# A feed-forward pair on one Trainium2 core: the second product in seven block products, its operand through DRAM

## The chip, the cores and the metric

The kernel runs on one core of a Trainium2 chip. The metric is the device time of one execution in microseconds (us). The engines are named as in the profile: PE is TensorE's matmul, PEld its weight load, DVE is VectorE, ACT ScalarE, POOL GpSimd, SP SyncE, which here issues all DMAs.

## What is computed

Three layers, one after the other, over 4 batches of 576 tokens and 512 channels: block-causal attention, a token and channel mixing layer with sines, and a low-rank layer with a feed-forward pair. The last layer is the one that the change touches:

```python
def _moe2_ref(x, U, V, w_ch1, w_ch2):
    xt = x.transpose(0, 2, 1)
    h = xt @ U @ V
    u = x + h.transpose(0, 2, 1)
    ch = np.maximum(u @ w_ch1, 0.0) @ w_ch2     # 512 -> 2048 -> 512
    return (u + ch).astype(np.float32)
```

`u` has 2304 tokens in all, `w_ch1` is 512 x 2048 and `w_ch2` 2048 x 512. The weights come as 64-bit floats, and each is decoded on the chip from its two 32-bit words.

## The kernel before

**Precision.** A factor of a matmul is held as two parts, a rounded high part and the rest (both fp32r, four bytes). A product of two factors is three matmuls: high by high, high by low, low by high. So the feed-forward pair costs, for every 128 x 128 block of a weight, three matmuls over the tokens.

**Stages.** For batch after batch the kernel runs attention (tiles `s`, `P`, `t`, `oA`, `oB`), then `theta` (`th`), `product` (`xp`), `mix` (`y`), `chan` (`c`), `lowrank` (`xq`, `G`) and `expand` (`h`). `expand` writes the finished `u`, transposed, to DRAM (`u3d`). The stages of one batch are woven into the attention of the next. The feed-forward pair comes last, and its first part fills the stages of the last batch, where no attention is left to weave in.

**The feed-forward pair.** Tokens are cut into five chunks of 512, 256, 512, 512, 512 (`CHUNKS`), hidden units into 16 tiles of 128 (`NF`). `ff1(n, f)` makes the hidden tile `m` of chunk n: 4 channel blocks by 3 matmuls, 12 in all, into one PSUM bank; ACT writes its rectified, rounded value and DVE the rest (`hh`). `ff2(n, f)` takes `hh` at once: 4 output blocks by 3 matmuls into four banks `acc`, which gather over all 16 f. So `m` and `acc` alternate, 12 matmuls each, and the hidden layer never leaves the chip. That makes 960 matmuls for each of the two products: 768 over 512 tokens and 192 over 256. At the end of a chunk POOL rebuilds u (`o`), DVE adds `acc`, and SP sends it out.

**Weights.** `load_f` brings a tile of either weight (`raw_w`, 512 KB), decodes it with two ACT and two DVE instructions of 512 columns (`d_w`), and splits it in two (`w`). All 32 tiles are on the chip before chunk 1 begins, in memory that attention, theta and mix have left.

**What sets the order.** The order is not written by hand. Every step gets a due time (`at_time`, with the table `CFG`), and a list scheduler (`Line.run`, with a price for each instruction in `Line.price`) simulates the engines, gives out buffers (`Line.home`, `fits`) and picks on each engine the ready step that is due first. `plan` repeats this with new priorities and keeps the best end. Some steps may go to one of several engines (`either`), and the scheduler picks one. `keep_warm` then puts dummy transposes (`t<-ident`, without a `P`) where the scheduled PE would idle in the first 140 us. The program on the chip follows the five resulting lists, each engine in its own order, so every recorded instruction bears the line of the recorder, L1195.

## Time and profile before

| | before |
|---|---|
| timed runs, median of 3 (lowest, highest) | 860.24 us (858.26, 861.49) |
| profiled execution, first to last instruction | 857.3 us |
| PE busy | 837.4 us, 98% of the span |
| DVE / ACT / POOL busy | 421.6 / 369.9 / 250.7 us |
| moved by DMA | 57.18 MB, 67 GB/s over the span |

The profile gives no time of the profiled execution besides its span. A share of busy time is a mean over the stages; the slices and windows below show it stage by stage. A PE matmul's duration in a group is the time from its start to its modelled end, and neighbours overlap, so the rate of PE is read from the chain of waits, where a piece such as "x12" spans from its first matmul's start to the next piece's start.

### The profile page before, as it was taken

Reading aid. Unit: us, or ns where it says so; the run is one execution under the profiler, and the core shown is the slowest. Engines: PE = TensorE matmul, PEld = TensorE weight load, DVE = VectorE, ACT = ScalarE, POOL = GpSimd, SP = SyncE. Lnnn points to the kernel's source line nnn. Section 1 sums busy time; section 2 is a strip of 40 time slices with the busy share of each in tenths; the row PEclk is TensorE's granted clock in tenths of the full one; section 3 lists DMA queues with packets and bytes.
Section 4 is the critical chain, followed back from the end, with each engine's and each line's share of the span. In section 5 each row is a group of like instructions: output and inputs, shape, how many; then the busy total and the mean of one; then the engine's idle time right before and its main releaser. Section 6 shows DMA issues by size and latency. Waiting matters only on the chain.

```text
span 857.3 us, 12606 instructions
## 1 busy us (share of the span) xinstructions
PE 837.4 (98%) x4882; PEld 687.3 (80%) x4882; DVE 421.6 (49%) x813; ACT 369.9 (43%) x856; POOL 250.7 (29%) x272
## 2 busy tenths in 40 slices
PE   8989899999999999999999999999999999999998
...
GB/s 216 189 171 114 107 58 59 45 45 30 101 31 31 45 16 57 107 134 83 160 84 105 196 99 0 154 2 75 1 0 1 50 1 0 1 50 0 1 1 49
DMA packets 41595, 57.18 MB, mean 67 GB/s; under 512 B 4672, under 2 KB 25664, under 8 KB 41536
## 3 DMA queue, kind: packets, MB, share of 16 engines
...
## 4 chain that ended last, share of the span: by engine, by line
PE 86%; DVE 6%; ACT 4%; DMA 1%; issue 1%; POOL 1%; SPq 0%; DVEq 0%; POOLq 0%; ACTq 0%
PE acc L1195 23%; PE m L1195 23%; PE y L1195 13%; PE c L1195 6%; PE th L1195 6%; PE t L1195 4%; PE s L1195 4%; PE oB L1195 3%; ACT P L1195 2%; DMA raw_th<-w_theta 1%; PE oA L1195 1%; PE G L1195 1%; DVE nm L1195 1%; PE xp L1195 1%; DVE P L1195 1%
## 5 line engine op out<-in xcount | busy, mean ns | idle before, releaser
L1195 PE MATMUL acc<-hh,w 128*128 128x512 f32 (+1 forms) x900 | 204.2, 373 | 0.5 <-DVE o L1195 0.2
L1195 PE MATMUL m<-us,w 128*128 128x512 f32 (+1 forms) x900 | 202.2, 372 | 0.0
L1195 PEld LDWEIGHTS acc<-hh,w 128*128 128x128 f32 x900 | 156.9, 188 | 32.9 <-DVE o L1195 1.5
L1195 DVE SCALAR_TENSOR_TENSOR hh<-m,hh 128x512 fp32r<-128x512 f32 (+1 forms) x80 | 50.9, 636 | 268.8 <-ACT hh L1195 268.8
L1195 PEld LDWEIGHTS m<-us,w 128*128 128x128 f32 x900 | 156.6, 188 | 30.3
L1195 ACT ACTIVATE hh<-m 128x512 fp32r<-128x512 f32 (+1 forms) x80 | 44.4, 554 | 297.4 <-PE m L1195 292.5
L1195 PE MATMUL y<-wtok,zh 128*128 128x288 f32 x576 | 120.4, 302 | 0.1
L1195 PEld LDWEIGHTS y<-wtok,zh 128*128 128x128 f32 x576 | 92.5, 189 | 4.0 <-issue 1.1
L1195 ACT ACTIVATE P<-s,nm 128x128 f32<-128x128 f32 (+2 forms) x144 | 79.0, 554 | 38.3 <-DVE nm L1195 36.8
L1195 PE MATMUL y<-wtok,zl 128*128 128x288 f32 x288 | 84.7, 297 | 0.0
L1195 PE MATMUL t<-ident,P 128*128 128x128 f32 x400 | 66.0, 284 | 10.1 <-ACT P L1195 3.3
L1195 PEld LDWEIGHTS t<-ident,P 128*128 128x128 f32 x400 | 47.3, 143 | 25.7 <-ACT P L1195 5.7
L1195 DVE TENSOR_REDUCE nm<-s 128x2 f32<-128x256 f32 (+4 forms) x80 | 64.1, 806 | 4.6 <-ACT P L1195 1.8
L1195 PE MATMUL s<-k,q 64*128 64x128 f32 (+4 forms) x320 | 64.9, 451 | 0.2 <-ACT P L1195 0.2
L1195 PE MATMUL c<-u,wch 128*128 128x288 f32 x384 | 59.1, 301 | 0.9 <-DVE xT L1195 0.9
L1195 PEld LDWEIGHTS c<-u,wch 128*128 128x128 f32 x384 | 53.4, 188 | 4.1 <-DVE xT L1195 1.9
L1195 POOL TENSOR_TENSOR o<-us,us 128x512 f32<-128x512 f32 x16 | 20.7, 1320 | 122.4 <-DVE o L1195 84.1
L1195 DVE TENSOR_TENSOR xT<-y,xT 128x288 f32<-128x288 f32 x64 | 29.0, 454 | 51.7 <-PE y L1195 51.4
L1195 PEld LDWEIGHTS y<-wtok,zl 128*128 128x128 f32 x288 | 53.9, 188 | 0.2
L1195 PE MATMUL th<-wth,xh 128*128 128x512 f32 x160 | 50.8, 399 | 0.1
L1195 PEld LDWEIGHTS s<-k,q 64*128 64x128 f32 (+1 forms) x320 | 30.4, 187 | 13.0 <-issue 7.1
L1195 ACT COPY PTB<-t 128x512 f32<-128x512 f32 (+3 forms) x63 | 27.7, 457 | 28.9 <-PE t L1195 28.2
...
## 6 DMA issues: line engine op xcount, KB each, us to landing
...
raw_tok<-wtokT SPq DMA_DIRECT2D x18, 288.0 KB, 3.2
...
k<-kT SPq DMA_DIRECT2D x16, 288.0 KB, 3.4
u3d<-xT SPq DMA_DIRECT2D x16, 288.0 KB, 2.1
outT<-o SPq DMA_DIRECT2D x16, 256.0 KB, 2.0
raw_th<-w_theta SPq DMA_DIRECT2D x8, 256.0 KB, 5.4
```

Source lines behind the costliest of these rows:

```text
L1195: fn(*[place(x) for x in args], **{k: place(x) for k, x in kw.items()})
```

## The change

`ff1` now works on one batch b (576 tokens) and a pair j of hidden tiles (eight pairs). The pair's output is seen as 2 x 2 blocks: two hidden tiles by two halves of 288 tokens. Each block is 12 matmuls over 288 tokens, a plain product. ACT or DVE rectify the blocks; DVE and POOL form the seven sums of blocks that the seven-product scheme (Strassen's, in Winograd's form) wants on the side of h. All seven, as plain fp32, go to DRAM (`hd`, 1.03 MB for each b and j, in four DMAs).

`load_w2` likewise forms the four sums on the side of w2 and splits all seven blocks of a pair of w2's tiles.

`ff2(b, s, j)` reads blocks of `hd` back (`hr`), splits them into two parts on the chip (`hv`) and multiplies: four products for s = 0 and three for s = 1, each 2 x 3 matmuls over 288 tokens. All eight PSUM banks hold the sums of one batch. `leave` combines them with u as each group of products ends. Counts: `ff1` has 4 x 8 x 48 = 1536 matmuls over 288 tokens, `ff2` 4 x 8 x 42 = 1344. The weights w1 are read in the fill as before, w2 only during the later `ff1`. All `ff2` steps come after all `ff1` steps.

```diff
-NA = 11
-CH = 384
-NCH = NT // CH
+NJ = NF // 2
+HW = DM // 2
...
-CFG = dict(L=60., d0=0., d1=0.84, d2=1.0, dec=1.8, T=13.68, P=13.88, R=25.74, I=29.568, X=2.61, m0=4., m1=72.64, w1=1., w2=2., w3=0.2, wx=24., po=0.5)
+CFG = dict(L=60., d0=0., d1=0.84, d2=1.0, dec=1.8, T=13.68, P=13.88, R=25.74, I=29.568, X=2.61, m0=4., m1=80., w1=1., w2=2., w3=0.2, u0=3., f1=150., f2=177., v0=0., v1=140.)
-LOC1 = "BBKKXTTTRRRRRRRB"
-LOC2 = "BBKKXTTTTTTKKKKB"
-CHUNKS = [512, 256, 512, 512, 512]
+NU = 4
+UX = (1,)
+EJ = 5
+NTW = 5
-LOOSE = {"pm": 1, "pa": 1, "hp": 1}
+LOOSE = {"pm": 1, "pa": 1, "F": 3, "G": 6}
-SLOWER = 1000.0
+SLOWER = {"-": 1000.0, "load_w1": 1000.0, "load_w2": 1000.0, "make_u": 300.0, "ff1": 300.0, "ff2": 300.0}
...
+    h3 = [[dram.tile([P, 7 * SH], F32, name=f"hd{b}_{j}") for j in range(NJ)] for b in range(B)]
...
+    for tag, n in {"U": NU, "W": NB, "G": NRX}.items():
+        for i in range(n):
+            line.home("w1p", f"{tag}e{i}", **{tag: ALL})
+    for i in range(4):
+        line.home("ps3", f"F{i}", F=ALL)
+        line.home("pp", f"pm{i}", pm=("s0",), F=("s0", "pm"))
+        line.home("ps", f"pa{i}", pa=(), F=("pa",))
...
     def load_w1(f):
+        t = line.tile([P, 2, DM], F32R, "W", f"w1_{f}")
+        w1t[f] = [t[:, a].rearrange("p (c f) -> p c f", c=NC4) for a in range(2)]
+        d = rawslot(f"d_w1_{f}")[:, :DM]
+        for g in range(2):
+            raw = rawslot(f"raw_w1_{f}_{g}")[:, :DM]
+            nc.sync.dma_start(raw.rearrange("p (c f) -> p c f", c=2), w1src[:, 2 * g:2 * g + 2, 2 * f * P:2 * (f + 1) * P])
+            unpack(raw, d[:, g * HW:(g + 1) * HW])
+        rnd("dh", t[:, 0], f32(d))
+        sub(t[:, 1], f32(d), t[:, 0], "dl")
...
+    def load_w2(j):
+        D = [halves(f"w2v{j}_{k}", U32, w=HW, tag="raw") for k in range(2)]
+        for k in range(2):
+            f = 2 * j + k
+            for v in range(2):
+                raw = rawslot(f"w2raw{j}_{k}{v}")[:, :DM]
+                nc.sync.dma_start(raw, w2[f * P:(f + 1) * P, v * DM:(v + 1) * DM])
+                unpack(raw, D[k][:, v])
+        D = [f32(d) for d in D]
+        sa, sb = [halves(f"w2S{j}_{a}", w=HW, tag="raw") for a in "ab"]
+        tt(sa[:, 0], D[0][:, 1], D[1][:, 1], ALU.add)
+        tt(sa[:, 1], sa[:, 0], D[0][:, 0], ALU.subtract)
+        tt(sb[:, 0], D[0][:, 1], D[0][:, 0], ALU.subtract)
+        tt(sb[:, 1], D[1][:, 0], sa[:, 1], ALU.subtract)
+        dst = wpairs(j)
+        for d, src in zip(dst, (D[0][:, 0:1], D[1], sa, sb)):
+            rnd("wh", d[:, :, 0], src)
+            sub(d[:, :, 1], src, d[:, :, 0])
...
-    def ff1(n, f):
-        u, w = us[n], CHUNKS[n]
-        hp = line.tile([P, 512], F32, "hp", f"m{n}_{f}", PSUM)
-        hp = hp[:, :w]
-        k = 0
-        for c in range(NC4):
-            for g, mv in ((0, 0), (0, 1), (1, 0)):
-                nc.tensor.matmul(hp, w1t[f][g][:, c, :], u[mv][:, c], start=(k == 0), stop=(k == 11))
-                k += 1
-        hh = line.tile([P, 2, max(CHUNKS)], F32R, "hh", f"hh{n}_{f}")[:, :, :w]
-        nc.scalar.activation(out=hh[:, 0], in_=hp, func=AF.Relu)
-        nc.vector.scalar_tensor_tensor(out=hh[:, 1], in0=hp, scalar=0.0, in1=f32(hh[:, 0]),
-                                       op0=ALU.max, op1=ALU.subtract)
-        hs[n, f] = hh
...
-    def ff2(n, f):
-        w = CHUNKS[n]
-        if f == 0:
-            accs[n] = [(abank(f"acc{n}_{d}") if d < PA else line.tile([P, 512], F32, "a3", f"acc{n}_{d}", PSUM))[:, :w]
-                       for d in range(NC4)]
-        hh = hs.pop((n, f))
-        for d in range(NC4):
-            ds_ = slice(d * P, (d + 1) * P)
-            for i, (g, mv) in enumerate(((0, 0), (0, 1), (1, 0))):
-                nc.tensor.matmul(accs[n][d], w2t[f][g][:, ds_], hh[:, mv],
-                                 start=(f == 0 and i == 0), stop=(f == NF - 1 and i == 2))
...
+    FIRST4 = (("A11", "B11", 0), ("S2", "T2", 1), ("S3", "T3", 2), ("S1", "T1", 3))
+    LAST3 = (("A12", "B21", 0), ("A22", "T4", 2), ("S4", "B22", 3))
+
+    def fbank(name):
+        return line.tile([P, 512], F32, "F", name, PSUM)[:, :SH]
+
+    def three(bank_, w, u, start, stop):
+        for i, (g, mv) in enumerate(((0, 0), (0, 1), (1, 0))):
+            nc.tensor.matmul(bank_, w[g], u[mv], start=start and i == 0, stop=stop and i == 2, skip_group_check=True)
+
+    def ff1(b, j):
+        n = f"{b}_{j}"
+        ha, hb, hc, hdd = [halves(f"{x}{n}", tag="G") for x in ("ha", "hb", "hc", "hd")]
+
+        def quarter(k, t):
+            bank_ = fbank(f"m{n}_{k}{t}")
+            w = w1t[2 * j + k]
+            ts_ = slice(t * SH, (t + 1) * SH)
+            for c in range(NC4):
+                three(bank_, [w[g][:, c] for g in range(2)], [uu[b][c][:, g, ts_] for g in range(2)], c == 0, c == NC4 - 1)
+            return bank_
+
+        relu(ha[:, 0], quarter(0, 0))
+        relu(hc[:, 1], quarter(1, 1))
+        m = quarter(0, 1)
+        nc.vector.scalar_tensor_tensor(out=ha[:, 1], in0=m, scalar=0.0, in1=ha[:, 0], op0=ALU.max, op1=ALU.subtract)
+        nc.sync.dma_start(hd[b][j][:, 0:2 * SH].rearrange("p (v c) -> p v c", v=2), ha)
+        nc.vector.scalar_tensor_tensor(out=hb[:, 1], in0=m, scalar=0.0, in1=hc[:, 1], op0=ALU.max, op1=ALU.subtract)
+        tt(hb[:, 0], hc[:, 1], ha[:, 1], ALU.subtract)
+        nc.sync.dma_start(hd[b][j][:, 2 * SH:4 * SH].rearrange("p (v c) -> p v c", v=2), hb)
+        relu(hc[:, 0], quarter(1, 0))
+        nc.sync.dma_start(hd[b][j][:, 4 * SH:6 * SH].rearrange("p (v c) -> p v c", v=2), hc)
+        tt(hdd[:, 0], hc[:, 0], hb[:, 0], ALU.subtract)
+        nc.sync.dma_start(hd[b][j][:, 6 * SH:], hdd[:, 0])
...
+    def ff2(b, s, j):
+        w = wv[j]
+        if s == 0:
+            group, at = FIRST4, ((0, 2, ("B11", "T1")), (2, 4, ("T2", "T3")))
+        else:
+            group, at = LAST3, ((4, 6, ("B21", "B22")), (6, 7, ("T4",)))
+        v = {}
+        for a, c, names in at:
+            k = c - a
+            raw = halves(f"hr{b}_{j}_{a}", n=k, tag="G")
+            nc.sync.dma_start(raw, hd[b][j][:, a * SH:c * SH].rearrange("p (v c) -> p v c", v=k))
+            t = line.tile([P, 2, 2, SH], F32R, "U", f"hv{b}_{j}_{a}")[:, :k]
+            rnd("hh", t[:, :, 0], raw)
+            sub(t[:, :, 1], raw, t[:, :, 0])
+            for i, x in enumerate(names):
+                v[x] = t[:, i]
+        for a, x, k in group:
+            for m in range(2):
+                if s == 0 and j == 0:
+                    accs[b, k, m] = fbank(f"acc{b}_{k}_{m}")
+                three(accs[b, k, m], [w[a][:, g, m * P:(m + 1) * P] for g in range(2)],
+                      [x_ for x_ in (v[x][:, 0], v[x][:, 1])], s == 0 and j == 0, j == NJ - 1)
+            if j == NJ - 1:
+                for m in range(2):
+                    leave(b, s, k, m)
...
+        r, ea, eb = evs[b, m]
+        acc = accs[b, k, m]
+        o11, o12, o21, o22 = [r[h][:, t * SH:(t + 1) * SH] for h in range(2) for t in range(2)]
+        s1, u2, u3, x = ea[:, 0], ea[:, 1], eb[:, 0], eb[:, 1]
+        if s == 0:
+            if k == 0:
+                nc.scalar.copy(s1, acc)
+            elif k == 1:
+                tt(u2, acc, s1, ALU.add)
+                tt(o12, o12, u2, ALU.add)
+                tt(o21, o21, u2, ALU.add)
+            elif k == 2:
+                tt(u3, acc, u2, ALU.add)
+                tt(o22, o22, u3, ALU.add)
+            else:
+                tt(o22, acc, o22, ALU.add)
+        elif k == 0:
+            tt(o11, acc, o11, ALU.add)
+        elif k == 2:
+            tt(o21, acc, o21, ALU.add)
+            nc.sync.dma_start(outT[(2 + m) * P:(3 + m) * P, b * S:(b + 1) * S], r[1])
+        else:
+            tt(o12, acc, o12, ALU.add)
...
+    first = [(b, j) for j in range(EJ) for b in (0, 1)] if MIX else [(b, j) for b in (0, 1) for j in range(EJ)]
+    for i, (b, j) in enumerate(first):
+        when = max(when, t1 + CFG["m1"] * i / len(first), nw[2 * j + 1] + 0.01)
+        feed(b, j, when)
+    t = max(tE, when)
+    late = [(b, j) for b in (0, 1) for j in range(EJ, NJ)] + [(b, j) for j in range(NJ) for b in (2, 3)]
+    for i, (b, j) in enumerate(late):
+        feed(b, j, t + CFG["f1"] * i / len(late))
+    for j in range(NJ):
+        at_time(tE + CFG["v0"] + CFG["v1"] * j / NJ, load_w2, j)
+    t += CFG["f1"]
+    step = CFG["f2"] / B / NJ / 7
+    for b in range(B):
+        for s in range(2):
+            for j in range(NJ):
+                at_time(t, ff2, b, s, j)
+                t += step * (3 if s else 4)
```

The order of the new program at the places that the prediction speaks of:

PE in the fill of the last batch before: `acc` of one hidden tile and `m` of the next alternate, 512 tokens a matmul (`hh` is the split hidden tile, `us` the split u, `w` a weight tile).

```order
L1195 MATMUL acc_0_4659<-hh_8_5599,w_8_5300 128x512 x3
L1195 MATMUL acc_1_4866<-hh_8_5599,w_8_5300 128x512 x3
L1195 MATMUL acc_2_4604<-hh_8_5599,w_8_5300 128x512 x3
L1195 MATMUL acc_3_4639<-hh_8_5599,w_8_5300 128x512 x3
L1195 MATMUL m_10_5675<-us_0_4221,w_10_0_5411 128x512
L1195 MATMUL m_10_5675<-us_1_4251,w_10_0_5411 128x512
L1195 MATMUL m_10_5675<-us_0_4221,w_10_1_5441 128x512
```

Four of the twelve blocks of `m` stand here. Each hidden tile is used as soon as it is split.

PE now, at the one place where `ff1` (`m`, from the split u `uf`) ends and `ff2` (`acc`, from the split blocks `hv` and the blocks of w2 `w2d`, `w2b`, `w2c`) begins.

```order
L1295 MATMUL m_7_10_7987<-uf_0_6836,w_15_5957 128x288 x3
L1295 MATMUL m_7_10_7987<-uf_1_6859,w_15_5957 128x288 x3
L1295 MATMUL m_7_10_7987<-uf_2_6892,w_15_5957 128x288 x3
L1295 MATMUL m_7_10_7987<-uf_3_6909,w_15_5957 128x288 x3
L1295 MATMUL acc_0_0_8013<-hv_0_0_7911,w2d_6001 128x288 x3
L1295 MATMUL acc_0_1_8018<-hv_0_0_7911,w2d_6001 128x288 x3
L1295 MATMUL acc_1_0_8025<-hv_0_2_7919,w2b_6155 128x288 x3
L1295 MATMUL acc_1_1_8030<-hv_0_2_7919,w2b_6155 128x288 x3
L1295 MATMUL acc_2_0_8036<-hv_0_2_7919,w2c_6177 128x288 x3
L1295 MATMUL acc_2_1_8044<-hv_0_2_7919,w2c_6177 128x288 x3
```

What alternated stands apart: 1536 `m` and then, without a break, 1344 `acc`, all of 288 tokens.

PE now, where the four products of the first batch end and the three begin (the last pair j = 7, then j = 0 and one group of j = 1).

```order
L1295 MATMUL acc_2_0_8036<-hv_7_2_8177,w2c_7991 128x288 x3
L1295 MATMUL acc_2_1_8044<-hv_7_2_8177,w2c_7991 128x288 x3
L1295 MATMUL acc_3_0_8051<-hv_7_0_8168,w2b_7857 128x288 x3
L1295 MATMUL acc_3_1_8057<-hv_7_0_8168,w2b_7857 128x288 x3
L1295 MATMUL acc_0_0_8013<-hv_0_4_8202,w2a_6124 128x288 x3
L1295 MATMUL acc_0_1_8018<-hv_0_4_8202,w2a_6124 128x288 x3
L1295 MATMUL acc_2_0_8036<-hv_0_6_8211,w2a_6124 128x288 x3
L1295 MATMUL acc_2_1_8044<-hv_0_6_8211,w2a_6124 128x288 x3
L1295 MATMUL acc_0_0_8013<-hv_1_4_8236,w2x_6591 128x288 x3
L1295 MATMUL acc_0_1_8018<-hv_1_4_8236,w2x_6591 128x288
L1295 MATMUL acc_3_0_8051<-hv_0_4_8202,w2c_6177 128x288 x3
L1295 MATMUL acc_3_1_8057<-hv_0_4_8202,w2c_6177 128x288 x3
```

Between the last matmul that `acc_3` gets from the four products and the next one that writes it stand 16 others: the groups of `acc_0` and `acc_2`, and 4 of the next pair that the scheduler pulled ahead.

DVE now, at the same place: what it does between two runs of splits (`ea`, `eb` hold partial sums, `o` is u on its way to the output).

```order
L1295 TENSOR_TENSOR eb_0_8304<-acc_2_0_8036,ea_0_8284 128x288
L1295 TENSOR_TENSOR eb_1_8309<-acc_2_1_8044,ea_1_8290 128x288
L1295 TENSOR_TENSOR o_1_8082<-o_1_8082,ea_1_8290 128x288
L1295 TENSOR_TENSOR o_3_8089<-o_3_8089,ea_1_8290 128x288
L1295 TENSOR_TENSOR o_2_8073<-o_2_8073,eb_0_8304 128x288
L1295 TENSOR_TENSOR o_3_8089<-o_3_8089,eb_1_8309 128x288
L1295 TENSOR_TENSOR o_2_8073<-acc_3_0_8051,o_2_8073 128x288
L1295 TENSOR_TENSOR o_3_8089<-acc_3_1_8057,o_3_8089 128x288
L1295 TENSOR_TENSOR hv_3_4_8311<-hr_3_4_8184,hv_3_4_8311 128x2x288
L1295 TENSOR_TENSOR hv_4_4_8352<-hr_4_4_8219,hv_4_4_8352 128x2x288
L1295 TENSOR_TENSOR hv_4_6_8372<-hr_4_6_8225,hv_4_6_8372 128x288
L1295 TENSOR_TENSOR hv_5_4_8388<-hr_5_4_8253,hv_5_4_8388 128x2x288
```

The second half of the output work reads `acc_3` behind eight other additions; before the change DVE had four additions at the end of a chunk.

PE before, in the attention of the second batch, after `oB` of its second head pair.

```order
L1195 MATMUL xp_4_1266<-ident,xd_1152 128x128 x4
L1195 MATMUL s_3_2_1277<-k_3_1009,q_3_999 128x384 x2
L1195 MATMUL t_2_0_1_1293<-ident 128x128 x4
L1195 MATMUL t_2_0_0_1298<-ident,P_2_0_1108 128x128
L1195 MATMUL t_2_0_1_1293<-ident 128x128 x2
L1195 MATMUL t_2_0_1_1293<-ident,P_2_0_1108 128x128
L1195 MATMUL t_2_0_0_1298<-ident,P_2_1_1129 128x128 x2
L1195 MATMUL t_2_0_1_1293<-ident,P_2_1_1129 128x128 x2
L1195 MATMUL xp_1_1328<-ident,xT_381 128x128 x4
L1195 MATMUL t_2_2_0_1340<-ident,P_2_2_1167 128x128 x3
```

There are 6 dummy transposes in these rows.

PE now, at the same place.

```order
L1295 MATMUL xp_4_1310<-ident,xd_1194 128x128 x4
L1295 MATMUL s_3_2_1321<-k_3_1048,q_3_1039 128x384 x2
L1295 MATMUL t_2_0_1_1349<-ident 128x128 x21
L1295 MATMUL t_2_0_0_1371<-ident,P_2_0_1161 128x128
L1295 MATMUL t_2_0_1_1349<-ident,P_2_0_1161 128x128
L1295 MATMUL t_2_0_0_1371<-ident,P_2_1_1174 128x128
L1295 MATMUL xp_1_1380<-ident,xT_426 128x128 x4
L1295 MATMUL t_2_0_0_1371<-ident,P_2_1_1174 128x128
L1295 MATMUL t_2_0_1_1349<-ident,P_2_1_1174 128x128 x2
L1295 MATMUL t_2_2_0_1401<-ident,P_2_2_1205 128x128 x3
```

The dummy transposes are now 21 in one piece, and 9 more follow before the first `y`; in the whole program 97 stand where 62 stood. The steps themselves stand in nearly the same order.

## Rows read from the trace of the kernel before

**Rows 1.** The page: busy time of the engines, and 40 slices of the span.

```profile
PE 837.4 (98%) x4882; PEld 687.3 (80%) x4882; DVE 421.6 (49%) x813; ACT 369.9 (43%) x856; POOL 250.7 (29%) x272
PE   8989899999999999999999999999999999999998
GB/s 216 189 171 114 107 58 59 45 45 30 101 31 31 45 16 57 107 134 83 160 84 105 196 99 0 154 2 75 1 0 1 50 1 0 1 50 0 1 1 49
```

**Rows 2.** Busy us by window: start:end, length, engines with (xinstructions), PE clock, DMA share, GB/s.

```profile
480.00:500.00 20.00, 20.00 (x89) 15.49 (x88) 19.31 (x31) 14.90 (x27) 3.07 (x4) 1.00 0.61 193
600.00:650.00 50.00, 50.00 (x216) 40.30 (x215) 6.22 (x9) 5.39 (x9) 0.00 (x0) 1.00 0.00 1
800.00:857.30 57.30, 53.60 (x231) 42.92 (x229) 8.96 (x13) 5.39 (x9) 0.00 (x0) 1.00 0.05 19
```

**Rows 3.** Chain of waits: start us, length us, what; matmuls of 512, 256, 288 columns.

```profile
499.52 2.80 PE m L1195 x12
496.72 2.80 PE acc L1195 x12
...
555.76 1.38 PE acc L1195 x12
557.13 1.42 PE m L1195 x12
...
450.85 6.34 PE c L1195 x48
457.19 6.41 PE y L1195 x48
463.60 3.27 PE c L1195 x24
```

**Rows 4.** Groups by shape, eviction, decode and split: engine, operation, shapes xcount | busy, mean ns | idle.

```profile
L1195 DVE TENSOR_TENSOR xT<-y,xT 128x288 f32<-128x288 f32 x64 | 29.0, 454 | 51.7 <-PE y L1195 51.4
L1195 DVE TENSOR_TENSOR w<-d_w,w 128x512 fp32r<-128x512 f32 x12 | 8.0, 682 | 0.0
L1195 DVE TENSOR_TENSOR us<-u,us 128x512 fp32r<-128x512 f32 x5 | 6.6, 1337 | 2.0 <-PE m L1195 2.0
L1195 DVE TENSOR_TENSOR u<-xT,u 128x288 fp32r<-128x288 f32 x9 | 4.4, 494 | 0.6 <-POOL u L1195 0.6
L1195 DVE SCALAR_TENSOR_TENSOR da_th<-da_th,raw_th 128x256 uint32<-128x256 uint32 x8 | 3.3, 420 | 0.6 <-ACT raw_th L1195 0.6
L1195 DVE TENSOR_TENSOR wtok<-da_tok,wtok 128x576 fp32r<-128x576 f32 x1 | 0.7, 745 | 0.0
L1195 POOL TENSOR_TENSOR w<-d_w,w 128x512 fp32r<-128x512 f32 x18 | 25.6, 1429 | 20.1 <-ACT w L1195 16.9 <-DVE w L1195 3.0
L1195 POOL TENSOR_TENSOR u<-xT,u 128x288 fp32r<-128x288 f32 x23 | 18.9, 824 | 11.5 <-ACT u L1195 5.4 <-DVE u L1195 4.9
L1195 POOL TENSOR_TENSOR o<-us 128x256 f32<-128x256 f32 x4 | 2.9, 738 | 0.0
L1195 ACT ACTIVATE wtok<-da_tok 128x576 fp32r<-128x576 f32 x1 | 0.7, 666 | 0.0
```

**Rows 5.** DMA: two windows as in Rows 2, then issues with KB and us to landing.

```profile
0.00:20.00 20.00, 16.42 (x103) 11.73 (x104) 11.57 (x33) 13.04 (x42) 6.24 (x13) 1.00 0.68 221
548.00:552.00 4.00, 3.92 (x31) 3.50 (x30) 3.76 (x8) 0.77 (x2) 4.00 (x5) 1.00 0.99 350
...
u3d<-xT SPq DMA_DIRECT2D x16, 288.0 KB, 2.1
u<-u3d SPq DMA_DIRECT2D x8, 256.0 KB, 3.3
```

**Rows 6.** The clock's fall: windows as in Rows 2, then PE's row of the timeline.

```profile
100.00:110.00 10.00, 6.70 (x31) 3.75 (x31) 9.67 (x21) 9.07 (x17) 7.37 (x9) 0.69 0.36 118
110.00:120.00 10.00, 9.91 (x65) 9.37 (x63) 8.04 (x16) 8.11 (x23) 6.40 (x7) 0.80 0.08 26
...
104.86 1.39 PE L1195 MATMUL t<-ident,P 128*128 128x128 f32 x4 [2.40 <-DVE P L1195]
```

**Rows 7.** Timeline of the end: start us, length us, engine, what.

```profile
847.89 5.71 PE L1195 MATMUL acc<-hh,w 128*128 128x512 f32 x24
851.64 2.74 DVE L1195 TENSOR_TENSOR o<-acc,o 128x512 f32<-128x512 f32 x4 [2.23 <-PE acc L1195]
852.36 2.38 SPq L1195 DMA_DIRECT2D outT<-o  x4
```

More of the change, by code (lines that the diff above doesn't have):

```diff
@@ L410, in run @@
                     best, f = min((max(t, free[f]) + y.cost, f) for f, y in x.ways.items())
-                    if f != e and best < t + way.cost - SLOWER:
+                    if f != e and best < t + way.cost - x.slow:
                         stash.append(item)
@@ L618, in abank, with wtile @@
         return line.tile([P, 512], F32, "pa", name, PSUM)
-    def wtile(name):
-        return line.tile([P, 2, DM], F32R, "K", name)
+    def wtile(name, tag):
+        return line.tile([P, 2, DM], F32R, tag, name)
     def toktile(name):
@@ L1004, in build @@
         spread(t0, t0 + CFG["X"], [(expand, b, d) for d in range(NC4)])
-    w1src = w1.rearrange("(c p) f -> p c f", p=P)
-    w1t, w2t = [None] * NF, [None] * NF
-    def btile(name, shape, dt):
-        return line.tile(shape, dt, "B", name)
-    def load_f(name, src, oh, ol):
-        raw = btile(f"raw_{name}", [P, 2 * DM], U32)
-        nc.sync.dma_start(raw if len(src.shape) == 2 else raw.rearrange("p (c f) -> p c f", c=NC4), src)
-        ta = rawslot(f"d_{name}", U32)[:, :DM]
-        decode([(raw.rearrange("p (c two) -> p c two", two=2), slice(0, DM))], ta, oh, ol)
@@ L1095, in pre_out @@
[L1095 to L1107 removed]
+    hd = [[line.fixed(h3[b][j], f"hd{b}_{j}") for j in range(NJ)] for b in range(B)]
@@ new lines, in tt, with relu @@
+    def tt(out, a, b, op):
+        if a.space == PSUM:
+            nc.vector.tensor_tensor(out=out, in0=a, in1=b, op=op)
+        else:
+            line.either(lambda: nc.gpsimd.tensor_tensor(out=out, in0=a, in1=b, op=op),
+                        lambda: nc.vector.tensor_tensor(out=out, in0=a, in1=b, op=op))
+    def relu(out, a):
+        line.either(lambda: nc.scalar.activation(out=out, in_=a, func=AF.Relu),
+                    lambda: nc.vector.tensor_scalar(out=out, in0=a, scalar1=0.0, scalar2=0.0, op0=ALU.max, op1=ALU.max))
@@ new lines, in halves, with unpack @@
+    def halves(name, dt=F32, n=2, w=SH, tag="RT"):
+        return line.tile([P, S], dt, tag, name)[:, :n * w].rearrange("p (v c) -> p v c", v=n)
+    w1src = w1.rearrange("(c p) f -> p c f", p=P)
+    w1t = [None] * NF
+    def unpack(raw, ta):
+        r = raw.rearrange("p (c two) -> p c two", two=2)
+        lo, hi = r[:, :, 0], r[:, :, 1]
+        nc.scalar.activation(out=f32(ta), in_=f32(hi), func=AF.Copy, scale=EXPFIX)
+        nc.scalar.activation(out=lo, in_=lo, func=AF.Copy, scale=LOFIX)
+        nc.vector.scalar_tensor_tensor(out=ta, in0=ta, scalar=3, in1=lo,
+                                       op0=ALU.logical_shift_left, op1=ALU.bitwise_or)
+        nc.vector.scalar_tensor_tensor(out=ta, in0=hi, scalar=SIGN, in1=ta,
+                                       op0=ALU.bitwise_and, op1=ALU.bitwise_or)
@@ new lines, in build, with wpairs @@
+    wparts, wv = {}, {}
+    def wpairs(j):
+        q, k = divmod(j, 2)
+        pair = [P, 2, 2, HW]
+        if q in LONE:
+            first = line.tile([P, 1, 2, HW], F32R, "W1", f"w2d{j}")
+        else:
+            if q not in wparts:
+                wparts[q] = line.tile(pair, F32R, "W", f"w2d{q}")
+            first = wparts[q][:, k:k + 1]
+        if j in INX:
+            x = xtile(f"w2x{j}", [P, 2, 2, 2, HW], F32R)
+            mid = [x[:, 0], x[:, 1], line.tile(pair, F32R, "W", f"w2c{j}")]
+        else:
+            mid = [line.tile(pair, F32R, "W", f"w2{a}{j}") for a in "abc"]
+        return first, *mid
@@ L1130, in build @@
[L1130 to L1148 removed]
+    tI = tT + 1.0 + CFG["P"] + CFG["R"]
```

181 lines of the change are left out of this document (72 added, 109 removed).

## The prediction, made before the changed kernel was run

> **What bounds the kernel now.** I read the busy line and the slices first [rows 1]. PE is busy 837.4 us of the span of 857.3, and its slices stand at 9 in all but the first and the last; DVE is busy 421.6 us, ACT 369.9, POOL 250.7. A share over the whole span hides stages, so the windows come next [rows 2]. In 600 to 650 PE is busy 50.00 of 50 us, DVE 6.22, ACT 5.39, POOL 0, and the DMA engines nothing; in 800 to the end it is much the same (53.60 of 57.30 us, with the tail). In 480 to 500, where `mix` and `chan` of the last batch are woven with the first chunk, PE is also full (20.00), and DVE nearly so (19.31). So from about 480 us on the time is the number of PE's matmuls by their rate, and 250 us of three engines lie unused near the end. That is what the change draws on: it pays PE work with DVE, ACT, POOL and DMA work.
>
> **The feed-forward matmuls.** The chain of waits gives the rate at each width [rows 3]. Twelve matmuls of 512 columns take 2.80 us, 233.3 ns each; twelve of 256 take 1.38 or 1.42 us, 115 to 118.8 ns, say 116.7. Before there are 768 `m` and 768 `acc` of 512 columns and 192 and 192 of 256: 1536 x 233.3 + 384 x 116.7 = 403.2 us. After there are 1536 `m` and 1344 `acc`, all of 288 columns. The trace of before has that width in other stages with the same pattern, a new weight load for each matmul: 48 `c` in 6.34 us, 132.1 ns; 48 `y` in 6.41, 133.5; 24 `c` in 3.27, 136.3 [rows 3]. A straight line through the 256 and 512 rows gives 116.7 + 32 x 116.6/256 = 131.2 ns. I take 132.1, the longest full-speed piece: 2880 x 132.1 = 380.4 us, **22.8 less**. The ends are 131.2 ns (377.9, 25.3 less) and 136.3 (392.5, 10.7 less); 133.5 would give 384.5, 18.7 less. Only the second product gets cheaper: an eighth of its half, some 25 us; the narrower matmuls give 2 of that back.
>
> **The new vector work beside `ff1`.** `ff1` and `ff2` now stand apart. The order lets me count what each engine does between the last eviction of `c` and the first `acc`. PE has 1104 `m` there and a few matmuls of `xq`, `G` and `h`, about 152 us. By the groups of before [rows 4], DVE has 63 decodes of 256 words at 420 ns (26.5 us), 52 evictions and rests from PSUM at 454 (23.6), 27 sums of 288 at 494 (13.3), 12 splits at 682 (8.2), and about 20 us in shorter or fewer ones (14 rectifications, 10 more of 420, 8 of 745, 6 from PSUM): 92 us. POOL has 30 at 738, 16 at 824 and 12 at 1429: 52.5 us with two inputs, 7 in others. ACT comes to about 67. None reaches 152, not even DVE and POOL one after the other (144.5). So PE should stay full; for in-order waits within a pair I add **2 us**, between 0 and 8. What hides them is the four `F` banks: PE is a bank or two ahead of the evictions.
>
> **The new vector work beside `ff2`.** PE has 1344 x 0.1321 = 177.5 us. DVE has about 91 splits of 2 x 288 at 745, 48 sums from PSUM at 454, 44 from SBUF at 494: 111 us. ACT has as many roundings at 666 and some copies, about 78 [rows 4]. There are eight `hv` tiles, so the splits run some four pairs ahead. At the join of `ff1` and `ff2` the last `m` and the first `acc` stand back to back; the first `hv` and the last block of w2 are made long before. No term.
>
> **The seams.** Within each of the four batches, at s = 0 to s = 1, the new first write of the bank `acc_3` follows its last one of the four products by 16 matmuls, 16 x 0.1321 = 2.11 us. It is no new start: the three products add onto the same bank only after DVE has taken the old sum away. DVE has by then queued `ea` and `eb` (4 from PSUM at 454), four sums in SBUF at 494, and only then the two that read `acc_3` (454). The last of `acc_2` stands 6 matmuls ahead of the end of `acc_3`, so DVE's four SBUF sums end about 2.2 us after that end, the read of `acc_3_0` about 2.65 after, that of `acc_3_1` about 3.1. PE wants the first at 2.11: a stall of 0.5 to 1 us at each of four seams. **3 us**, between 0 (if the reads go out early) and 6. Behind the reads on DVE stand splits of `hv`, which have four pairs of cover. From batch to batch the next sums take banks that have long been read: 0.
>
> **DMA.** h goes out, 1.03 MB for each of 32 (b, j), 33.0 MB, and comes back, 33.0. In the stretch of `ff1` I count 38.8 MB (h out 23.7, w2 8.4, u 3.5, early reads of h 3.2) in 152 us, 255 GB/s; in `ff2` 39.2 MB (29.8, u again 4.7, output 4.7) in 178 us, 220 GB/s. In the trace of before the queue moved 350 GB/s at a share of 0.99 for 4 us with transfers of the same kind and size, and 221 GB/s at a share of 0.68 for the first 20 us; a 288 KB transfer landed 2.1 us after its issue [rows 5]. By both windows the engines' ceiling is 325 to 350 GB/s, so I take the transfers as hidden, at a share of 0.7 to 0.8. They have no price as long as reads run ahead; the cover is thinner than for any other term.
>
> **The first 400 us.** The steps and their order are the same. The planner fills 97 dummy transposes where it filled 62, 24 of the 35 more at one place, where PE before idled 2.40 us behind DVE's `P` and the clock then stood at 0.69 and 0.80 in two windows of 10 us, which together are some 10 us at the lower level, 1.2 GHz [rows 6]. If the fill keeps PE at 2.4 GHz there, at most 5 us come back; if the dummies are in the way, each for no longer than a matmul of 256 columns [rows 3], 35 x 0.115 = 4 us are lost. I take **1 us less**, between 5 less and 4 more. At the end four evictions and four transfers gave 3.7 us behind the last matmul [rows 7]; now the last are two, of 288 columns, and a transfer of 288 KB: 0.
>
> **Sum.** Against the profiled execution: 857.3 - 22.8 + 2 + 3 - 1 = 838.5. The median of the runs is 2.9 us above that span (860.24 to 857.3), which I carry over: 841.4, **841.5 us**.
>
> **Rivals.**
>
> *DVE becomes the bound of `ff1`.* The split of `us` on DVE beside POOL took 1337 ns, that of `w` of the same size without POOL 682 [rows 4], 1.96 times as long. If that befell every DVE operation with two SBUF inputs there (31.7 us and the decode's 26.5), DVE would have 92 + 56 = 148 us, and with a tenth lost to waits in order 163: some 12 us more than PE's 152, 854. Against it: POOL is busy only 60 of the 152 us, so that the whole factor cannot fall on all. The Trainium skill ("SBUF — State Buffer", section "SBUF: two separate sides") says that a DVE operation with two SBUF inputs and a GpSimd one shut each other out for a whole instruction; by that rule alone the two queues add up to 144.5 us at most and still fit, and the row of 1337 agrees with it.
>
> *The transfers become the bound, slower than before.* If long stretches go no faster than the best slice of before, 216 GB/s [rows 1], `ff1` takes 38.8/0.216 = 179.6 us, 27.6 more, and `ff2` 181.5, 4 more: 873. The point from which it decides is a rate of about 255 GB/s in `ff1`, and it turns slower than before by over 0.5% under some 223 GB/s. For it: SP issues in order, so that a `hd` that waits for DVE holds up reads behind it, and no row shows a rate over 221 for longer than 4 us. Against it: those windows were not short of queue, but of work. The Trainium skill (the same page, section "The DMA setup-cost knee") gives about 2 us for each transfer beside its bytes at 436 GB/s; taken one after another, transfers of 288 KB would run at 110 GB/s by an estimate from that page, and the 78 MB of both stretches would take some 709 us. The window of 350 GB/s contradicts that for several transfers in flight.
>
> *The clock comes back.* The fill works in full and the first part gains 5 us, and the rate is that of the line, 131.2 ns (2.5 us less), with the seams hidden: 841.5 - 4 - 2.5 - 2 = 833.
>
> *The change does not do what it says.* The order settles it: 1536 and 1344 matmuls of 288 columns stand in it.
>
> **How the numbers follow.** The forecast has 0.68, DVE as the bound 0.12, the transfers 0.08, the clock 0.12. Less than 0.5%, 4.3 us, can hardly be told from no change. Faster by more than that (under 855.9) are the forecast, the clock and over half of the DVE case: 0.87. Within 0.5% lies the rest of it: 0.05. Slower (over 864.5) is the transfers' case: 0.08. The range runs from the clock's 833 to 857, which takes in the rate of 136.3 ns (853.5) and the DVE case.
>
> **What would show it.** In the changed profile's chain `m` and `acc` should stand in pieces of x12 with 1.59 us; the first `acc` should begin some 181 us ahead of the end, PE without a gap to its left; ahead of the first new `acc_3` in each batch PE should idle under 1 us behind DVE; the DMA share should be 0.7 to 0.8 in the last 330 us. The forecast is wrong if PE idles in `ff1` behind DVE's or POOL's sums (the first rival), or in either stretch behind `hr` or for a free `ha` to `hd` tile (the second), or if the windows after 100 us show the lower clock at another place than before.

## The result

The changed kernel takes 850.25 us (median of 4 runs, 847.5 to 852.07), the kernel before, in the same comparison, 859.68 (median of 4, 858.26 to 861.49). The ratio is 0.989, with a 95% interval of 0.9865 to 0.9916. The forecast was 841.5 in a range of 833 to 857: faster, as forecast, but by 9.4 us where 18.7 were expected. The profiled execution has a span of 845.7 us, 11.6 below the 857.3 of before.

The page after: busy line, slices of what the DMA engines moved, two groups of transfers.

```profile
PE 822.2 (97%) x5877; PEld 740.3 (88%) x5877; DVE 538.9 (64%) x1105; ACT 451.1 (53%) x1057; POOL 268.5 (32%) x323
...
GB/s 213 180 179 127 107 61 125 67 46 31 102 32 31 46 2 73 1 100 155 151 141 105 137 175 262 234 239 332 240 237 217 302 222 283 173 303 144 298 135 57
...
hr<-hd SPq DMA_DIRECT2D x96, 288.0 KB, 4.7
hd<-hc SPq DMA_DIRECT2D x32, 288.0 KB, 2.6
```

Against [rows 1], DVE is busy 117 us more, ACT 81 and POOL 18, and the last sixteen slices but one move 135 to 332 GB/s, where most had 0 to 2. PE is 15 us less busy and still at 97% of the span.

Windows after, with the columns of [rows 2]: three that answer to those, then the stretch of `ff1` alone and that of `ff2`.

```profile
480.00:500.00 20.00, 19.89 (x150) 19.65 (x149) 8.52 (x19) 5.80 (x14) 6.88 (x10) 1.00 0.31 102
600.00:650.00 50.00, 50.00 (x379) 50.00 (x378) 31.13 (x67) 24.19 (x60) 25.66 (x29) 1.00 0.70 236
690.00:728.00 38.00, 38.00 (x288) 38.00 (x287) 20.80 (x34) 17.83 (x29) 0.00 (x0) 1.00 0.71 239
...
504.00:658.80 154.80, 153.57 (x1139) 151.18 (x1138) 96.64 (x205) 64.25 (x153) 60.45 (x73) 1.00 0.74 253
658.80:840.90 182.10, 179.86 (x1345) 178.72 (x1343) 107.67 (x186) 78.72 (x130) 11.20 (x13) 1.00 0.63 211
```

The new vector work lies under a full PE in both stretches. The chain of waits after has hardly anything else than PE in its last 260 us. Shown are the stretch of `m`, the first of `acc`, and the short step through DVE that stands between the two groups of products of a batch (start us, length us, what).

```profile
577.42 81.41 PE m L1295 x612
658.84 24.73 PE acc L1295 x186
683.57 0.04 issue
683.61 0.45 DVE eb L1295
684.05 2.31 DVE o L1295 x4
686.36 0.23 issue
686.60 0.45 DVE o L1295
687.05 0.04 issue
687.09 42.04 PE acc L1295 x314
```

From start to start these 612 matmuls of `m` are 132.8 ns apart.

Where did the rest of the gain go? I added up, over the whole trace, the time from the start of each PE instruction to the next. The `m` and `acc` of before come to 403.6 us, those of after to 388.5: 15.1 less. All else on PE, and the end, grew by 3.5, so the span shrank by 11.6. The experiments take these two numbers apart.

### The profile page after: what moved, and what is told of

Read it like the earlier page. It is cut to its first block, busy times and chain, and to the rows that moved or that the text cites. A ratio compares the mean times of both kernels' runs of the same rounds, so it can differ in the third digit from the quotient of the medians.

```text
span 845.7 us, 16102 instructions
## 1 busy us (share of the span) xinstructions
PE 822.2 (97%) x5877; PEld 740.3 (88%) x5877; DVE 538.9 (64%) x1105; ACT 451.1 (53%) x1057; POOL 268.5 (32%) x323
## 5 line engine op out<-in xcount | busy, mean ns | idle before, releaser
L1295 PE MATMUL m<-uf,w 128*128 128x288 f32 x1536 | 213.9, 296 | 0.7 <-POOL uf L1295 0.4
L1295 PEld LDWEIGHTS m<-uf,w 128*128 128x128 f32 x1536 | 207.1, 188 | 2.3 <-POOL uf L1295 0.9
L1295 ACT ACTIVATE hv<-hr 128x576 fp32r<-128x576 f32 x126 | 78.3, 624 | 96.0 <-PE acc L1295 80.6
L1295 DVE TENSOR_TENSOR hv<-hr,hv 128x576 fp32r<-128x576 f32 (+1 forms) x124 | 81.9, 688 | 67.2 <-ACT hv L1295 63.9
L1295 PE MATMUL t<-ident,P 128*128 128x128 f32 x400 | 63.3, 278 | 7.1 <-DVE PTA L1295 1.8
L1295 PE MATMUL acc<-hv,w2c 128*128 128x288 f32 x384 | 61.7, 296 | 2.2 <-DVE o L1295 2.2
L1295 PEld LDWEIGHTS acc<-hv,w2c 128*128 128x128 f32 x384 | 54.3, 188 | 3.2 <-DVE o L1295 3.2
L1295 POOL TENSOR_TENSOR o<-o,ea 128x288 f32<-128x288 f32 x8 | 6.3, 812 | 151.2 <-DVE ea L1295 151.2
L1295 POOL TENSOR_TENSOR hb<-hc,ha 128x288 f32<-128x288 f32 x24 | 19.8, 826 | 81.9 <-DVE ha L1295 45.4
L1295 ACT ACTIVATE hc<-m 128x288 f32<-128x288 f32 x49 | 19.9, 408 | 47.2 <-PE m L1295 43.5
```

What stands on the lines that cost most here:

```text
L1295: fn(*[place(x) for x in args], **{k: place(x) for k, x in kw.items()})
```

## The experiments

### The seam: what PE waits for between four products and three

A seam is the place in a batch where the four products end and the three begin. DVE at the first seam, in the changed kernel (start us, length us, engine, line, operation, out<-in), and PE's wait there.

```profile
683.24 0.81 DVE L1295 TENSOR_TENSOR eb<-acc,ea 128x288 f32<-128x288 f32 x2
683.97 1.35 DVE L1295 TENSOR_TENSOR o<-o,ea 128x288 f32<-128x288 f32 x2
685.25 1.43 DVE L1295 TENSOR_TENSOR o<-o,eb 128x288 f32<-128x288 f32 x2
686.60 0.81 DVE L1295 TENSOR_TENSOR o<-acc,o 128x288 f32<-128x288 f32 x2
...
687.09 1.07 PE L1295 MATMUL acc<-hv,w2c 128*128 128x288 f32 x6 [0.59 <-DVE o L1295]
```

Four sums within SBUF stand between `eb` and the reads of `acc_3`, as the order showed. From start to start PE loses 0.71 to 0.75 us there and 0.10 on the next matmul, at each of four seams: 3.3 us in all. `acc3_first` moves the reads forward on DVE, after the planner is done:

```diff
+        first = [next(o for o in order if o.eng == DVE_ and f"acc{b}_3_{m}" in names(o)) for m in range(2)]
...
+        late = [o for o in order[i + 1:j] if o.eng == DVE_ and o not in first]
...
+        order = rest[:j + 1] + late + rest[j + 1:]
```

> The changed kernel with one thing moved: in each batch DVE takes the two sums that read acc_3 right behind those that read acc_2, and the four sums within SBUF come behind them. Theory (PE waits at the seam because DVE's queue has four other sums ahead): the four gaps of 0.71 to 0.75 us and the 0.10 behind each, 3.3 us together, are gone, PE runs through from the first acc to the last, and the time falls by 3.3 us, from 850.3 to about 847. Rival (the gap is the hand-over of a PSUM bank itself, whatever stands ahead on DVE): the gaps stay over 0.5 us and the time stays within 1 us of 850.3.

Measured: 846.35 us (843.48 to 847.03), 3.9 less than the changed kernel, ratio to the kernel before 0.9849 (0.9827 to 0.987). Its DVE at the same place, and the last step of its chain on PE:

```profile
685.20 0.81 DVE L1309 TENSOR_TENSOR eb<-acc,ea 128x288 f32<-128x288 f32 x2
685.95 0.86 DVE L1309 TENSOR_TENSOR o<-acc,o 128x288 f32<-128x288 f32 x2
686.72 1.43 DVE L1309 TENSOR_TENSOR o<-o,ea 128x288 f32<-128x288 f32 x2
...
688.07 0.81 DVE L1309 TENSOR_TENSOR o<-o,eb 128x288 f32<-128x288 f32 x2
...
660.80 176.79 PE acc L1309 x1329
```

1329 `acc` now run in one piece without a step through DVE, and no gap is left. That the seam was DVE's order and not the hand-over of a bank is shown. In the trace all `acc` come to 178.63 us where the changed kernel has 181.95, 3.3 less. The spans of the two traces differ by only 1.4 us (845.7 and 844.3): in the stretches ahead of the first seam, where the order of every engine is the same in both, `acc3_first` lost 2.0 more. Differences of this size between single traces say nothing.

### The products alone: seven undone

`classic` keeps the separate stages, h through DRAM and the width, and makes eight plain products. The planner arranges the whole program anew for it (PE's order differs from 10 us on), and leaves out the 35 added dummy transposes:

```diff
-        for a, x, k in group:
-            for m in range(2):
...
+        for d in range(4):
+            h, m = divmod(d, 2)
+            for t in range(2):
...
+                for k in range(2):
+                    w = wv[j][k]
+                    three(accs[b, d, t], [w[:, h, g, m * P:(m + 1) * P] for g in range(2)],
+                          [v[k][:, t, 0], v[k][:, t, 1]], j == 0 and k == 0, j == NJ - 1 and k == 1)
```

> The changed kernel with the seven products undone and all else kept: h still goes out to DRAM and comes back, but as its four plain blocks, w2 is split as four plain blocks, and ff2 makes eight products of blocks, 48 matmuls for each b and j where 42 stood. Theory (the seven products save 192 matmuls of PE and cost it only the seams): the stretch of acc is 1536 x 133.05 = 204.4 us without gaps, where the changed kernel has 182.2; the stretch before it is as long as now; the time is about 850.3 + 22.2 = 872, less 3.8 if the planner leaves out the 35 added dummies. Rival (the seven products' sums, splits and transfers also cost PE some 4 us between 360 and 560 us): the excess in that window goes with them, and the time is about 864 to 868.

Measured: 873.67 us (871.97 to 875.78), 23.4 more than the changed kernel. The whole second product is one piece of its chain:

```profile
662.76 203.72 PE acc L1250 x1536
```

That is 132.6 ns a matmul, and 203.7 - 178.6 = 25.1 us more than the seven products take without their seams, an eighth of 203.7 (25.5) within 0.4. So the saving in products is all there; what the missing dummies do to the median is under 1 us by the runs on the fill below. The rival finds no support: the waits between 360 and 610 us (defined below) are 8.6 us in `classic` and 8.3 in the changed kernel. As far as one trace each can tell, the sums, splits and transfers of the seven products cost PE nothing there.

### The width: the kernel before in chunks of 288

```diff
-CHUNKS = [512, 256, 512, 512, 512]
+CHUNKS = [288] * 8
```

> The kernel before with eight chunks of 288 tokens in place of 512, 256, 512, 512, 512, and nothing else changed: classical, h on the chip, m and acc in turn, 3072 matmuls of 288 columns. It prices the width alone. By the rate that the changed kernel showed (133.05 ns) the pair takes 408.7 us where it took 403.6: 5.1 us more, some 864. By the rate of the prediction (132.1 ns) 405.8, 2.2 more, 861. By the upper end of the prediction (136.3 ns) 418.7, 15 more, 874. The end of the program may give 1 us back, since the last chunk is shorter.

Measured: 875.46 us (874.39 to 876.31), 16.3 more than before (859.15 in the same comparison), above all three values that I had expected, the highest (874) too. Its chain late in the program shows the rate, and its waits on PE between 380 and 520 us what else came (what was waited for, us in total, times, longest).

```profile
728.23 1.60 PE m L1195 x12
729.83 1.60 PE acc L1195 x12
...
PE acc L1195 <- ACT hh L1195: 2.1, 4, 0.7
PE acc L1195 <- DVE hh L1195: 1.1, 1, 1.1
```

1.60 us for twelve is 133 ns, the rate of the changed kernel, so nothing slower than that is behind it. But `m` and `acc` together take 415.0 us against 403.6. By rate alone, 3072 at 132.8 ns, they would take 408.0; before, by the rates below, 401.1. So 6.9 us are rate and 4.5 are waits within the pair. There are 128 hidden tiles in place of 80, and 1.60 us in place of 2.8 to split one while PE works on another; `acc` waits for `hh` where before it did not. The other 5.3 us of the 16.7 in the spans (874.0 and 857.3) lie outside the pair, most of them in the stages. The planner arranged this program anew as well (PE's order differs from 44 us on), so how much of these waits belongs to the width and how much to the order that it found is not shown. The rate of before I had read a little too high. A row of its chain, and a window of 240 us:

```profile
686.82 2.73 PE acc L1195 x12
...
600.00:840.00 240.00, 240.00 (x1036) 194.27 (x1035) 36.35 (x53) 26.25 (x44) 13.66 (x11) 1.00 0.03 9
```

Most pieces of twelve take the 2.80 us of [rows 3], 233.3 ns a matmul, which the forecast took; but others take 2.72 to 2.79. The 1034 matmuls of 512 columns that start in this window (the row counts two more that began before it) are 232.0 ns apart. Those of 256 columns are some 116.5 apart.

### The fill and the clock

`fill_as_before` leaves 24 dummy transposes out of the changed kernel, `before_fill_more` puts 24 into the kernel before:

```diff
+                    if o.start > 90e3:
+                        count = min(count, 6) if o.start < 100e3 else 0
```

```diff
+                    if o.start > 90e3 and count > 0:
+                        count = 28 if count > 3 else count
```

> The changed kernel with 24 of its 97 dummy transposes left out: 6 remain at the place near 100 us, where the kernel before has 6, and none behind. Theory A (the fill holds PE's clock): without it the granted clock between 100 and 120 us falls to about 0.75 in every run, as in the profile before; 24 x 0.109 = 2.6 us of dummies go, about 4.6 us come in at half clock, so the span of the profile is some 2 us over 845.7. Theory B (the dummies stand in the way and the clock falls or not by chance): the clock of the runs is spread as it was (0.994 to 1.0), and the median falls by some 2.6 us to about 847.6.

> The kernel before with 24 more dummy transposes at the one place near 100 us where PE idles 2.40 us behind P and the clock falls (28 in one piece where 4 stood), as the changed kernel has them. Theory A (the dummies keep the clock up there): the windows of 100 to 120 us show a granted clock near 1.0 where before showed 0.69 and 0.80; 4.6 us come back, 24 x 0.109 = 2.6 us are paid, and the time falls by 2 us, to about 856.7. Theory B (they only stand in the way): the clock falls as before, and the time grows by up to 2.6 us, to about 861.3.

Measured: 849.39 us for the first (849.33 to 849.78; the changed kernel 850.25), 858.58 for the second (856.59 to 860.43, 12 runs; before 859.15; ratio 0.999, interval 0.998 to 1.0). Windows of 100 to 120 us in the columns of [rows 6]: the changed kernel, then `fill_as_before`, then `before_fill_more`.

```profile
100.00:110.00 10.00, 7.67 (x62) 5.98 (x59) 9.85 (x24) 9.97 (x19) 7.41 (x9) 1.00 0.36 112
110.00:120.00 10.00, 9.92 (x76) 9.44 (x75) 8.65 (x19) 8.93 (x23) 6.41 (x7) 1.00 0.19 57
```

```profile
100.00:110.00 10.00, 6.78 (x39) 4.75 (x36) 9.49 (x23) 9.97 (x19) 7.24 (x9) 0.76 0.36 116
110.00:120.00 10.00, 9.81 (x59) 9.36 (x58) 7.20 (x17) 8.05 (x19) 4.80 (x5) 0.73 0.08 27
```

```profile
100.00:110.00 10.00, 8.17 (x63) 6.10 (x62) 9.95 (x22) 9.10 (x17) 6.95 (x9) 1.00 0.36 120
110.00:120.00 10.00, 9.37 (x71) 8.75 (x70) 9.48 (x20) 9.28 (x26) 6.85 (x7) 1.00 0.08 28
```

With the dummies PE stays at 2.4 GHz in these two executions, without them part of both windows is at 1.2 GHz, and the mean clock is 0.993 to 0.995 in all four runs of `fill_as_before`. Theory A is right for the clock. But in other executions with the same dummies it fell a little (`acc3_first`, below 1 in both windows: 0.91 and 0.92; `weave`, 1.00 and 0.83), and the mean clocks of the changed kernel's four runs are 1.0, 0.996, 0.996 and 0.994, with spans of 845.7, 849.1, 847.8 and 850.3. In the traces the attention of the last batch ends 1.8 and 2.2 us earlier with the 24 dummies than without. They themselves take some 2.6 us, so the clock gave back 4.4 to 4.8 in these executions, and less in others. In the medians leaving them out gained 0.9 us in the one kernel and putting them in gained 0.6 in the other, less than can be told.

`acc3_fill` has both edits, the seam's and the fill's.

> acc3_first with the fill of fill_as_before: the seam's wait removed and the 24 later dummies left out. If the two add up (3.9 us and 0.9 us against the changed kernel's 850.25), the median is about 845.5; the windows of 100 to 120 us show the lower clock as fill_as_before did. If the dummies do save the clock in enough runs to pay for themselves, it is 846.5 or more.

Measured: 846.0 us (844.97 to 847.02), ratio 0.984 (0.9827 to 0.9853). The two do not add up clearly: it is the same as `acc3_first` within the spread of either, and the clock of the two windows fell as expected (0.75 and 0.74). These two are the fastest of all.

### The room in the transfers

`hd_twice` issues each transfer of h to DRAM twice, the second to a place that nobody reads:

```diff
+                o.call = o.call + [(fn, (View(t.buf, None, F32, args[0].steps), args[1]), kw)]
```

> The changed kernel with every transfer of h to DRAM issued twice, the second into a region that nobody reads: 33 MB more, all in the stretch of ff1. Theory (the transfers are hidden now and their ceiling is 325 to 350 GB/s): from 500 to 660 us 62.5 MB would have to move where 38.8 do, at 403 GB/s in 155 us; at the ceiling that takes 179 to 192 us, so PE idles 24 to 38 us and the time is 874 to 888. Rival 1 (a sustained rate of only 260 GB/s, so that the change stands at the edge): 62.5 MB take 240 us, and the time is over 925. Rival 2 (there is more room than the rows show): no more than 3 us.

Measured: 876.38 us (873.94 and 878.81), 26.1 more, in the theory's range. Two windows of it and one of the changed kernel, then what its PE waits for between 500 and 720 us.

```profile
580.00:620.00 40.00, 37.15 (x269) 36.92 (x268) 17.43 (x40) 10.27 (x26) 8.40 (x11) 0.96 0.99 349
620.00:660.00 40.00, 38.04 (x280) 37.02 (x279) 20.18 (x49) 15.30 (x41) 16.93 (x20) 1.00 0.98 354
```

```profile
580.00:620.00 40.00, 40.00 (x304) 40.00 (x303) 26.85 (x64) 20.12 (x51) 16.36 (x21) 1.00 0.76 256
```

```profile
PE m L1304 <- POOL uf L1304: 8.7, 3, 5.5
PE G L1304 <- ACT x2h L1304: 2.8, 3, 1.9
PE acc L1304 <- DVE hv L1304: 2.7, 2, 1.7
PE m L1304 <- DVE hb L1304: 2.3, 2, 1.2
```

The engines' ceiling is 349 to 354 GB/s over 80 us; the changed kernel needs 253 of it. In the traces `m` and `acc` take 24.9 us more. What PE waits for longest is not h itself but the reload of u (`uf`), which stands in SP's order behind the added writes.

### The stages between 360 and 610 us

From start to start, in pieces of over 0.14 us beyond a matmul's own rate, PE of the kernel before loses 4.2 us in this stretch and that of the changed kernel 8.3. These sums move by up to 0.8 with how a matmul's own rate is set, and the changed kernel and `acc3_first` (9.2) run the same order here, so differences of about 1 us say nothing. Its waits there:

```profile
PE G L1295 <- ACT x2h L1295: 1.3, 2, 0.7
PE y L1295 <- DVE xT L1295: 0.6, 1, 0.6
PE c L1295 <- DVE xT L1295: 0.4, 1, 0.4
PE m L1295 <- POOL uf L1295: 0.4, 2, 0.2
```

`G` waits twice now, in the low-rank stages of the third batch (456 us) and of the fourth (555); in the kernel before PE waited so once, at 542. `weave` pulls matmuls ahead of it on PE (`low` holds the last two `G` and some `h` of a batch, and `pull` puts n ready `y`, `m` or `c` ahead of each):

```diff
+        for o, n in zip(low, (9, 4, 10, 2, 2, 2, 2, 3, 3) if b == 2 else (9, 4, 5)):
+            pull(o, n)
```

> The kernel acc3_first with one more move, on PE alone: in the low-rank stages of the third and the fourth batch, near 455 and 554 us, 8 to 9 matmuls of y and m that stood behind the last G are done ahead of it, while ACT and DVE split its operand, and some more ahead of the first h. Theory (PE waited there for x2h and x2l, 1.5 us at the one place and 1.5 at the other, because the stages of a batch and ff1 are woven too thinly): the waits of G go, of which the h behind them may take 1 us again, and the time falls by 1.5 to 2 us against acc3_first's 846.35. Rival (the work that is pulled ahead is itself only just ready, or is missed behind): PE waits as long elsewhere in 440 to 580 us and the time stays.

Measured: 850.95 us (848.9 to 852.78), 4.6 more than `acc3_first`. The wait of `G` is gone, and others took its place:

```profile
PE h L1334 <- DVE xT L1334: 1.3, 4, 0.5
PE m L1334 <- DVE uf L1334: 1.3, 1, 1.3
PE c L1334 <- DVE xT L1334: 1.1, 2, 0.6
```

The sum of the stretch went from 9.2 to 10.9. The rival holds: what was pulled ahead is missed between the `h` behind, and some of it was not ready either. This fits a stretch that is short of ready work rather than badly ordered at one place, though it does not prove it. Another 1.7 us of the difference lie ahead of 360 us, where both programs are the same: that part is chance.

Three other settings of the planner, each with the seam's edit:

```diff
-MIX = 0
+MIX = 1
```

```diff
-EJ = 5
+EJ = 4
```

(and 6 in the third.)

> acc3_first with one setting of the planner changed: in the fill, ff1 of the first two batches takes turns pair by pair in place of one batch after the other. Counts, widths and the first 350 us stay. PE's waits between 360 and 600 us (time from start to start over a matmul's own rate, pieces over 0.14 us) are 4.2 us in the kernel before, 8.3 in the changed one and 9.2 in acc3_first. Theory C (these waits are a matter of which order the planner happens to find): they move by 2 us or more with the setting, and the time with them, 846.35 plus or minus 2 to 4. Theory D (they belong to the separate stages, since no acc fills the low-rank stages): they stay within 1.5 us of 9.2 and the time within 1.5 of 846.35.

> acc3_first with another setting changed: four pairs of hidden tiles of the first two batches are put into the fill where five were. Theory C: the waits between 360 and 600 us move by 2 us or more against 9.2, and the time with them. Theory D: they stay within 1.5 us, as does the time against 846.35.

> As ej4, with six pairs in the fill. Theory C: the waits between 360 and 600 us move by 2 us or more against 9.2. Theory D: within 1.5 us.

Measured, waits between 360 and 610 us and time: 10.4 and 848.0 for the first, 11.9 and 850.5 with four pairs, 11.1 and 848.7 with six; `acc3_first` 9.2 and 846.35. Neither theory holds alone. The order moves the waits by up to 2.7 us, and the time with them (C, with four pairs), but each of the kernels with separate stages has 8.3 to 11.9 us, none comes near the 4.2 of before (D). Why the kernel before has so much less is not settled: there `acc` and `m` of 512 and 256 columns fill these stages, and `before_288`, which has both but at 288, loses 11.1.

## Why the forecast was right in its direction and off in its size

**What adds up to 9.4.** The runs can be put in a row: before 859.2 -> chunks of 288, 875.5 (+16.3) -> separate stages, h through DRAM, still eight products, 873.7 (-1.8, less than the 4.2 that one setting of the planner moved) -> seven products, 850.3 (-23.4). So the seven products gave what they should, and what they need took some six tenths of it back. In the changed kernel the width costs 382.5 us against 15/16 of 401.1, that is 6.5, in rate alone (table), and 3.5 us of waits of the stages come on top. The forecast had the price of the width as 2 us, in the words "the narrower matmuls give 2 of that back", and those waits at nothing. These are the terms that were mis-sized; the mechanism, fewer matmuls under a full PE with the vector work and the transfers hidden, was right.

| term of the sum | forecast, us | measured, us | by |
|---|---|---|---|
| `m` and `acc` by count and rate | -22.8 | -18.6 | 232.0 and some 116.5 ns before (401.1), 132.8 after (382.5) |
| other waits of `m` and `acc` | +2 | +0.2 | 2.7 after, 2.5 before |
| seams | +3 | +3.3 | trace, `acc3_first` |
| first 360 us | -1 | -1.0 | trace; by estimate clock -4.6, 35 dummies +3.8, rest -0.2 |
| waits of the other stages, 360 to 610 | 0 | +3.5 | remainder |
| end | 0 | +1.0 | last PE start to end of span: 4.1 before, 5.1 after |
| span | -18.8 | -11.6 | 857.3 to 845.7 |

**The rate** was mis-sized from both sides: 233.3 for 512 columns came from one piece of twelve where the mean is 232.0, and 132.1 for 288 from the lowest of three pieces, called the longest though 48 `y` took longer (6.41 us). Each is 0.5% of 400 us, 2 us. The range of the rate, 131.2 to 136.3, held the 132.8.

**Luck.** The 2 us for waits within the pair came to 0.2 and hid part of this. And the first 360 us came out as forecast in the profiled execution alone: nearly all of the clock's 5 us and of the dummies' 4 came, and the difference is small by chance of that execution.

**The stages.** That PE would wait in the low-rank stages of two batches was not seen. That it does so because `acc` no longer fills them is not shown: `before_288` has `acc` there and loses more. The words "for in-order waits within a pair I add 2" looked for waits in the stretch of `ff1` alone, where there are none to speak of (153.57 of 154.80 us busy).

**The end** takes 1 us more, which the forecast put at 0. Its rows beside [rows 7]:

```profile
838.97 2.45 DVE L1295 TENSOR_TENSOR o<-acc,o 128x288 f32<-128x288 f32 x6 [6.49 <-PE acc L1295]
840.25 1.88 SPq L1295 DMA_DIRECT2D outT<-o  x4
```

From DVE's last sum (841.4) to the end are 4.3 us, where before had 2.9: the four transfers, now of 288 KB in place of 256, go out within 1.88 us where they took 2.38, the last two behind the very last sums. Which of this costs the 1.4 us no run takes apart.

**The vector work** was right: 92, 67 and 59.5 us forecast for DVE, ACT and POOL beside `ff1`, 96.64, 64.25 and 60.45 measured; beside `ff2` 111 and 78 forecast for DVE and ACT, 107.67 and 78.72 measured. PE waits for none of it outside the seams. So the rival with DVE as the bound did not come. Its mechanism is visible, with a price only at the seams: the sums `o<-o,eb` took 752 ns each there, beside POOL's, against the 494 of [rows 4], and so the four of a seam took 2.6 us, not 2.0. By these rows some 0.6 of the 0.71 to 0.75 us that PE waits at a seam is that, an estimate. In `acc3_first` two of the same sums that start after POOL's work take 0.81 us together. The Trainium skill ("SBUF — State Buffer", section "SBUF: two separate sides") says that such pairs exclude each other; these rows agree in direction.

**The transfers** were right: 253 GB/s beside `ff1` (255 forecast) and 211 beside `ff2` (220), at shares of 0.74 and 0.63. `hd_twice` shows that the rival stood a factor of 1.4 away. One transfer was not quite hidden, a reload of u in the chain of the changed kernel (3.3 us is the median of its kind):

```profile
569.64 6.98 DMA u<-u3d
...
576.70 0.68 POOL uf L1295
```

PE waited 0.4 us behind it, and 0.7 in `acc3_first`. The estimate from the Trainium skill ("SBUF — State Buffer", section "The DMA setup-cost knee") of 110 GB/s for transfers of this size one after another does not apply: several were in flight (by an estimate some four, from 4.7 us to landing at 236 GB/s), and 354 GB/s were measured.

**The clock** came back in the profiled execution, as in the third rival, but not in all runs. The median stands 4.55 us above the profiled span, where 2.9 were carried over from before: each run's time is about 1.8 us above its own span, and the profiled execution was the shortest of the four. It had the highest mean clock too, but two runs at 0.996 differ by 1.3 us, so the clock is not all of the spread.
